# One block of ones for both buffers of k and v, value sums in three buffers in turn, and a new list of units, in an attention and bilinear kernel

## The chip, the cores and the metric

The kernel runs on one core of one Trainium2 chip. The metric is the device time of one execution in microseconds; a run gives one such time, and the profile is taken from one execution.

## The reference

```python
a    = exp(phi - max(phi, axis=2));  a = a / (sum(a, axis=2) + 1e-9)     # phi: 8 x 8 x 576 x 32
k_m  = einsum('bhsm,bhsd->bhmd', a, k);  v_m = einsum('bhsm,bhsd->bhmd', a, v)
attn = softmax(q @ k_m^T / sqrt(64))                                     # 576 x 32 for each batch and head
x    = (attn @ v_m).transpose(0, 2, 1, 3).reshape(4608, 512)
out  = ((x @ w_a) * (x @ w_b)) @ w_out                                   # 512 x 1536, 512 x 1536, 1536 x 512
```

There are 8 batches, 8 heads, 576 tokens, a head of 64, 32 memory slots; q, k and v are 8 x 8 x 576 x 64. Everything goes in and out as float32.

## The kernel before

The kernel keeps three weights in SBUF in half precision (`wa_sb`, `wb_sb`, `wo_sb`) and takes the eight batches one after the other, overlapped. Its work is cut into units, and a string `PLAN` lists all of them in one order. The kernel goes through that string, and each engine carries out its own instructions in the order in which the string brings them; nothing reorders them. So the list sets which instruction stands behind which on every engine and on POOL's DMA queue.

The tokens of the list are these (a leading digit is the batch).

- `w..`, `o`, `p`, `k`, `v`, `q` issue a load from POOL's queue: weights, `w_out`, phi, k, v, q.
- `exp` (ACT) is the exponential of phi. `kv` (`kv_sums`, PE, L323) multiplies it with k, v and a block of ones in one go of 72 matmuls on small tiles (192 columns: 64 of k, 64 of v, 64 equal sums), `km` (DVE) divides by the sums, `kvt` transposes (PE, DVE).
- `qt`/`qh` (DVE) transposes q, `sc`/`sh` (PE) gives scores, `e`/`eh` (ACT, L425) their exponentials `E`. Batches 0 to 3 are normalised with slots on partitions: `den` (PE L465, and the logarithm on ACT L466), `nr` (ACT L476, and the product `A`, L478, on DVE for batches 0 and 1 and on POOL for 2 and 3). Batches 4 to 7 transpose instead (`ed`, `sm`, `tn`, `ad`, DVE).
- `v{n}{a,b}` (`fold`, PE L516, small tiles) multiplies v_m with a third of `w_a` or `w_b`, and `x..` (`take_fold`, L548) copies the result to `vab`. So x itself is never built: an up product is `A` times `vab`.
- `a b.i.h` and `b b.i.h` (`up_half`) are the up products of row block i and half h of the tokens: two matmuls each (L727); `a` is copied by ACT (L731), `b` is multiplied with that copy by the DVE (L734) into `ht`.
- For batches 5 to 7 the first eight of twelve row blocks take both halves by seven products instead of eight: `P b.i.k` (`seven`, PE L750), k being the product's number. Products 1, 6, 7 and 4 are added up in one PSUM bank (y) in that order, 5 and 3 in a second (v), 2 alone in a third (x). ACT copies products 1, 5 and 6 out (`z`, L755), the DVE adds such a copy to products 3, 7 and 2 (`ah`, `bh`, `al`, L759) and multiplies product 4 (L777); `H` and `J` do the last multiplication on POOL or DVE (L781). These need sums of `vab` and of `A`: `S` (`v_sum`, L533) and `T` (`a_sum`, L541), with P or D at the end for POOL or DVE.
- The down products (`two_downs`, L654) do the same for two blocks of 128 tokens at a time: seven products of six matmuls of 256 columns; `d n` carries out the next n matmuls of them, 756 in all. They need sums of `ht`, `h` on POOL or `g` on DVE (`sum_tokens`, L638, 128x768), and of `wo_sb`, `T` on POOL or `V` on DVE without a leading batch (`sum_weights`, L621, 128x768). ACT copies (`u`, L661), the DVE adds and writes `o_sb` (L665), SP stores it.
- `O` and `M` write constants; `M` is the block of ones of the second buffer, by POOL (L792).

k and v of even batches lie in `kv_sbs[0]`, of odd ones in `kv_sbs[1]`, each of three planes: k, v, ones. The value sums have three tiles, one for each third of the weights' columns (`vsum0`, `vsum1`, `vsum2`); the transposed k_m and v_m of batch 0 and the reciprocals of batches 0 to 3 borrow two of these.

Of the kernel before, what the change touches and what calls it, by code (L numbers as in the profile page):

```python
# [8 lines left out]
F32 = mybir.dt.float32  # L9
F16 = mybir.dt.float16  # L10
# [3 lines left out]
P = 128  # L14
# [4 lines left out]
wb0:256 0qt0 wa0:256 0qt3 wb256:512 0qt1 wa256:512 p1 0exp0 0exp1 F1 0ks0 0kt0 0ks1 0vs1 0vt1 0vs0 0vt0 M k1 F1  # L19
0hv0a 0s0 v1 0qt2 O 0kt1 0e0 F1 0s1 0e1 0hx0a0 0hx0a1 F2 0den10 0den01 0den11 0den00 wa512:1024 0hv0b 0hx0b0 0hx0b1  # L20
0hv1b 0nr01 0nr10 0hx1b1 0nr11 0nr00 0hv1a 0hx1a0 q1.0 wb512:1024 0hx1a1 F4 a0.0.1 1exp1 a0.0.0 b0.0.0 0hx1b0 a0.1.1
b0.0.1 1exp0 a0.3.1 b0.1.1 a0.3.0 a0.2.0 b0.3.1 b0.2.0 a0.2.1 b0.2.1 1kv a0.1.0 1km1 wa1024:1536 1km0 b0.3.0 q1.1
1kvt 0v1a 0x1a0 0x1a1 1v0a 1v1a 1v0b 1x1a0 1x0a0 1x0b0 a0.5.1 1x1a1 1qh20 wb1024:1536 b0.1.0 o1 a0.6.0 1qh30 a0.4.0
1qh10 1qh00 o0 o3 1sh0 1eh00 0v1b 1v1b 1x0b1 1eh10 1x0a1 0x1b0 1den00 0x1b1 1x1b1 o4 1den10 o2 a0.6.1 b0.6.0 b0.6.1
b0.5.1 1nr10 1nr00 1x1b0 b0.4.0 a0.7.1 b0.7.1 a0.7.0 a0.5.0 b0.7.0 a1.5.0 b0.5.0 h0.3 b1.5.0 a1.3.0 1qh21 a0.4.1 o5
b1.3.0 1qh31 1qh01 a1.4.0 b0.4.1 a1.1.0 1qh11 a1.2.0 b1.4.0 a1.0.0 b1.1.0 1sh1 0v2a 1eh01 1eh11 0x2a1 b1.0.0 0x2a0
b1.2.0 1den01 a1.6.0 0v2b 0x2b0 0x2b1 b1.6.0 v2 a0.9.1 1v2b 1v2a 1x2b0 1x2b1 a0.11.1 1x2a1 1x2a0 b0.9.1 a0.10.1
a0.9.0 b0.11.1 b0.10.1 b0.9.0 V20 1den11 a1.10.0 b1.10.0 a0.11.0 b0.11.0 a0.8.0 a1.11.0 b0.8.0 b1.11.0 1nr11 d1
1nr01 a0.10.0 d1 V00 a1.8.0 b0.10.0 a1.7.0 d1 b1.8.0 p2 V21 a1.11.1 b1.7.0 b1.11.1 d1 a1.3.1 a1.0.1 a1.2.1 g0.0 d1
b1.3.1 a1.6.1 d1 b1.2.1 b1.0.1 V01 a0.8.1 V10 a1.4.1 a1.9.0 d1 k2 2exp0 2exp1 g0.1 d1 V11 b1.6.1 V31 a1.5.1 p3 g0.2  # L30
b0.8.1 q2 d1 b1.4.1 d3 a1.1.1 b1.9.0 d6 2kv 3exp0 k3 d2 2km0 d1 a1.9.1 2km1 v3 d3 b1.5.1 d1 3exp1 d1 a1.10.1 d2
a1.8.1 2kvt b1.1.1 d2 h1.0 a1.7.1 2qt1 d4 2qt0 2qt3 2v1b 2x1b1 2v0a 2x1b0 T30 2qt2 2x0a1 d12 2x0a0 d4 g2.0 g1.1 2sc
g1.2 2e0 b1.7.1 d1 2e1 g1.3 q3 d2 b1.8.1 d3 b1.10.1 d1 2den0 d1 g2.1 p5 2den1 d1 b1.9.1 d1 2nr0 d5 2v2b 3kv 2v1a
g2.3 2x2b1 3km0 2nr1 2x2b0 2x1a1 d7 3km1 d6 3qt2 2x1a0 2v0b 2v2a 2x0b1 3qt3 d3 3qt0 2x2a1 d3 a2.6.0 d1 b2.6.0 d1
3qt1 a2.4.0 2x2a0 b2.4.0 d1 h2.2 d1 a2.7.0 d2 a2.4.1 d1 2x0b0 b2.4.1 d4 a2.3.0 a2.1.1 3kvt 5exp1 v5 b2.7.0 p4 b2.3.0
a2.8.0 b2.1.1 k5 a2.1.0 d2 a2.2.0 d2 q4 d1 a2.5.0 h3.3 3sc 3e0 d2 b2.2.0 d1 3e1 d2 b2.8.0 5exp0 d1 b2.1.0 v4 d2
a2.10.0 d2 b2.10.0 a2.0.1 a2.11.0 b2.11.0 b2.5.0 3den0 a2.0.0 d1 b2.0.1 h3.0 d1 g3.1 a2.5.1 d1 a2.9.0 k4 b2.5.1 h3.2
b2.0.0 3nr0 a2.11.1 d1 a2.8.1 b2.9.0 d1 3den1 d2 a2.10.1 d2 b2.10.1 d1 3v0a 3nr1 3x0a1 5kv 3x0a0 3v0b 3x0b0 b2.8.1
a2.2.1 d1 q5 d1 4qt0 b2.11.1 4qt3 4exp1 d1 3x0b1 d3 b2.2.1 d1 a2.9.1 d1 4qt1 d2 4qt2 d1 a2.7.1 b2.9.1 g4.3 d1 a2.6.1
h4.0 a2.3.1 d1 g4.1 d1 a3.3.0 d1 h4.2 4exp0 k7 b2.7.1 a3.2.0 d2 b2.6.1 d5 b3.3.0 b3.2.0 d2 4kv p6 3v2a 4km0 d2 3x2a1  # L40
4km1 d11 3x2a0 b2.3.1 d2 4kvt d2 a3.0.0 a3.3.1 v6 5km0 q6 d2 a3.1.0 5km1 k6 h5.0 d5 b3.1.0 a3.1.1 4sc 4e0 b3.0.0 d1
5qt3 d2 b3.1.1 5qt0 d1 a3.0.1 4e1 d3 b3.3.1 d5 3v1b 3v1a 4ed 3v2b 3x1b1 d5 3x1a0 d2 3x1a1 4sm0 d1 5qt1 d2 h5.3 3x2b0
5kvt a3.8.0 4sm1 d1 3x1b0 h5.1 3x2b1 d4 5qt2 d3 a3.6.1 b3.0.1 a3.10.0 d3 a3.4.0 d1 p7 d1 6exp1 d1 b3.8.0 b3.4.0 d1
a3.5.0 b3.6.1 d1 b3.10.0 4tn1 a3.7.0 a3.9.0 h5.2 d1 5sc 4tn0 5e0 d1 b3.5.0 5e1 a3.5.1 a3.11.0 d1 b3.7.0 d3 6qt0 d4
4v0a 4x0a0 4v1b 4v0b 4x0b1 d2 4x1b1 d5 6qt2 d1 4ad d1 5ed d1 a3.4.1 5sm0 b3.5.1 d2 b3.9.0 d1 4x1b0 d3 4x0a1 b3.11.0
# [38 lines left out]
def kernel(  # L84
# [196 lines left out]
    def units(b):  # L281
# [269 lines left out]
        def one(f, *a):  # L551
            return lambda: f(*a)
# [289 lines left out]
```

## Time and profile before

| | |
|---|---|
| median of 3 runs | 234.72 us (234.55 to 235.18) |
| span of the profiled execution | 232.1 us |
| PE busy | 214.1 us, 92% of the span, 2906 matmuls |
| DVE busy | 195.7 us, 84% |
| ACT busy | 169.4 us, 73% |
| POOL busy | 138.2 us, 60% |
| read and written in HBM | 42.47 MB and 9.44 MB |

The profiled execution's own span is 232.1 us; the time of a run holds some 2.6 us more than the span. In the profile, PE is the matrix engine (PEld loads its weights), DVE the vector engine, ACT the scalar engine, POOL the GpSimd engine and SP the engine that issues the stores. A row of a timeline gives the start and the length in microseconds, the engine, the line of the kernel, the operation, output and input names and sizes, and in square brackets how long the engine had idled and what released it. Consecutive instructions of one kind are put together (x6); the start of the next row, not the sum of lengths, tells how far apart they are, for matmuls overlap. A row of the groups gives the number of instructions, their busy time, the mean of one in nanoseconds, and the idle time ahead of them.

### The profile page before, as it was taken

The numbers are of one execution on the slowest core, as the hardware profiler recorded it, in microseconds if no ns is written. First come the engines' busy times: TensorE is split into PE (matmuls) and PEld (weight loads), VectorE is DVE, ScalarE is ACT, GpSimd is POOL, SyncE is SP. The second block draws the span as 40 slices with busy tenths as digits, with TensorE's granted clock in tenths as the row PEclk, the third lists the DMA queues.
The fourth block names the chain that finished last, engine by engine and source line by source line (L and its number), as shares of the span: only waits on it lengthen the run. The fifth ranks groups of instructions, "written<-read, shape, count | busy, mean of one in ns | idle before, by whom it ended". The sixth has DMA issues, their size and how long they took to land.

```text
span 232.1 us, 7493 instructions
## 1 busy us (share of the span) xinstructions
PE 214.1 (92%) x2906; PEld 163.6 (70%) x2906; DVE 195.7 (84%) x517; ACT 169.4 (73%) x450; POOL 138.2 (60%) x139
## 2 busy tenths in 40 slices
PE   1189879999999998999999999999999999999993
PEld 0143537588778777777777787887778877888882
DVE  3543899999987667898988999999999999999942
ACT  2206679987899997589978996977897769785330
POOL 7927233812549597893374099499475991881151
PEclk9999999999999999999999999999999999999999
DMA  6999999999998999999840902121303303032164
GB/s 229 238 199 256 205 205 205 205 259 258 208 284 138 264 207 243 253 241 254 210 93 4 190 1 65 28 64 32 93 3 90 78 16 92 18 77 55 42 158 111
DMA packets 26259, 34.09 MB, mean 147 GB/s; under 512 B 2000, under 2 KB 20304, under 8 KB 26224
## 3 DMA queue, kind: packets, MB, share of 16 engines
q0 software_dynamic: 19760, 23.14, 53.5%
q1 hardware_dynamic: 5952, 9.70, 16.2%
q10 hardware_dynamic: 512, 0.79, 1.0%
q8 instruction: 22, 0.36, 0.6%
q14 instruction: 13, 0.11, 0.1%
HBM read 42.47 MB, written 9.44 MB: 224 GB/s over the span
## 4 chain that ended last, share of the span: by engine, by line
PE 71%; DMA 17%; POOL 6%; ACT 3%; issue 2%; DVE 1%; POOLq 0%
PE py L654 18%; PE pb L727 11%; PE pa L727 11%; PE pv L654 9%; DMA wb_sb<-in_moe_w_b_dram 6%; DMA kv_sb<-in_k_dram 6%; PE py L750 5%; PE px L654 4%; PE pva L516 4%; DMA kv_sb<-in_v_dram 4%; PE pv L750 3%; POOL h_sums L638 2%; PE pkv L323 2%; PE px L750 1%; ACT vab L548 1%
## 5 line engine op out<-in xcount | busy, mean ns | idle before, releaser
L734 DVE TENSOR_TENSOR ht<-a_sb,pb 128x288 f16<-128x288 f16 (+2 forms) x144 | 60.5, 445 | 9.6 <-PE pb L727 5.3
L727 PEld LDWEIGHTS <-vab 128*128 128x128 f16 x576 | 55.3, 98 | 14.9 <-issue 2.4
L731 ACT CAST a_sb<-pa 128x288 f16<-128x288 f32 (+2 forms) x144 | 55.1, 417 | 13.6 <-PE pa L727 8.9
L727 PE MATMUL pb<-A,vab 128*128 128x288 f16 (+2 forms) x288 | 54.9, 286 | 0.1
L727 PE MATMUL pa<-A,vab 128*128 128x288 f16 (+2 forms) x288 | 54.3, 286 | 0.5 <-DVE A L478 0.4
L548 ACT CAST vab<-pva 128x512 f16<-128x512 f32 x82 | 45.4, 611 | 6.9 <-PE pva L516 6.8
L654 PEld LDWEIGHTS <-h_sums 128*128 128x128 f16 x432 | 41.4, 98 | 9.9 <-issue 2.4
L638 POOL TENSOR_TENSOR h_sums<-ht 128x768 f16<-128x768 f16 x19 | 31.2, 1645 | 21.4 <-DVE ht L734 21.3
L654 PE MATMUL py<-w_sums,h_sums 128*128 128x256 f16 x216 | 38.1, 273 | 0.0
L654 PEld LDWEIGHTS <-ht 128*128 128x128 f16 x324 | 31.2, 98 | 7.5 <-issue 2.2
L654 PE MATMUL pv<-wo_sb,h_sums 128*128 128x256 f16 x216 | 36.4, 273 | 0.0
L638 POOL TENSOR_TENSOR h_sums<-ht,h_sums 128x768 f16<-128x768 f16 x10 | 16.4, 1640 | 11.6 <-DVE h_sums L638 11.5
L755 ACT COPY z<-py 128x288 f32<-128x288 f32 x48 | 19.2, 415 | 2.3 <-PE py L750 1.8
L781 POOL TENSOR_TENSOR ht<-ah,bh 128x288 f16<-128x288 f16 x19 | 13.7, 737 | 10.1 <-DVE ah L759 7.1
L654 PE MATMUL px<-wo_sb,ht 128*128 128x256 f16 x108 | 18.9, 273 | 0.0
L654 PE MATMUL py<-wo_sb,ht 128*128 128x256 f16 x108 | 18.8, 273 | 0.0
L654 PE MATMUL py<-w_sums,ht 128*128 128x256 f16 x108 | 18.4, 273 | 0.0
L661 ACT ACTIVATE u<-py 128x256 f32<-128x256 f32 x36 | 14.4, 399 | 4.0 <-PE py L654 3.9
L425 ACT ACTIVATE E<-pscore 128x288 f16<-128x288 f32 x28 | 9.8, 431 | 9.5 <-PE pscore L412 9.4
L291 ACT ACTIVATE exp_sb<-phi_sb 128x576 f16<-128x576 f32 x16 | 10.9, 692 | 5.2 <-DMA phi_sb<-in_phi_dram 5.2
L300 DVE STREAM_TRANSPOSE qT<-q_sb 128x288 f32<-128x288 f32 x28 | 12.2, 456 | 2.6 <-DMA q_sb<-in_q_dram 2.6
L750 PE MATMUL py<-asum,vab 128*128 128x288 f16 x48 | 13.5, 286 | 0.0
(106 smaller groups left out, 383.0 us busy)
## 6 DMA issues: line engine op xcount, KB each, us to landing
out_dram<-o_sb SPq DMA_DIRECT2D x68, 128.0 KB, 2.4
phi_sb<-in_phi_dram POOLq DMA_DIRECT2D x8, 576.0 KB, 10.3
kv_sb<-in_v_dram POOLq DMA_DIRECT2D x8, 576.0 KB, 11.2
kv_sb<-in_k_dram POOLq DMA_DIRECT2D x7, 576.0 KB, 13.5
q_sb<-in_q_dram POOLq DMA_DIRECT2D x6, 576.0 KB, 11.9
wo_sb<-in_moe_w_out_dram POOLq DMA_DIRECT2D x6, 256.0 KB, 14.0
wa_sb<-in_moe_w_a_dram POOLq DMA_DIRECT2D x2, 512.0 KB, 14.2
wb_sb<-in_moe_w_b_dram POOLq DMA_DIRECT2D x2, 512.0 KB, 16.6
```

The lines of the kernel that those rows point to most:

```text
L291: nc.scalar.activation(out=t["exp"][:, 2 * z:2 * z + 2, :, :], in_=phis[b][:, 2 * z:2 * z + 2, :].rearrange("p c (i m) -> p c i m", m=M), ...
L300: nc.vector.transpose(out=t["qT"][:, hp, :].bitcast(F32), in_=qs[b][:, hp, :].bitcast(F32))
L548: engine_copy(out=vabs[b][z][:, g, lo:hi], in_=pva[:, 0:hi - lo])
L638: engine.tensor_tensor(out=out, in0=in0, in1=in1, op=op)
L654: nc.tensor.matmul(po, lhs[:, i], rhs[:, i], start=first and i == 0, stop=i == KH - 1, skip_group_check=not first)
L661: nc.scalar.mul(out=x, in_=po, mul=scale)
L727: nc.tensor.matmul(ps, vabs[b][x][:, g, P * i:P * (i + 1)], attn[b][:, g, ts], start=(g == 0), stop=(g == 1))
L731: nc.scalar.copy(out=a_sbs[b, i, hf][:, :n], in_=ps)
L734: nc.vector.tensor_tensor(out=ht[:, i, t0:t0 + n], in0=a_sbs.pop((b, i, hf))[:, :n], in1=ps, op=ALU.mult)
L750: nc.tensor.matmul(x[bank][0], lhs, rhs, start=first, stop=True, skip_group_check=True)
L755: nc.scalar.copy(out=x[name], in_=po)
L781: engine.tensor_tensor(out=ht[:, i, t0 + HALF:t0 + S], in0=x["ah"], in1=x["bh"], op=ALU.mult)
```

## The change

There are three edits.

First, k and v of both buffers and one plane of ones lie in one tile of five planes, k0 v0 ones k1 v1. Each `kv` reads three neighbouring planes; in odd batches the ones come first, and `take_kv` picks the columns accordingly. The write of the second plane of ones (`M`) is gone.

Second, the value sums (and the two borrowers) take their tile from a pool of three buffers in turn.

Third, the list is new from end to end. The units are the same, but their order differs, and some sums change engine: `V20` and `V00` become `T20` and `T00` (POOL), the token sums on POOL go from 34 to 40, and of the 24 value sums POOL does 10 (12 before) and the DVE 14 (12). The helpers `part_sums`, `take_part` and `part_transpose` are added, and no token of the list calls them; `slot_sums`, which no token called, is removed.

```diff
 PLAN = """
-... 0vs1 0vt1 0vs0 0vt0 M k1 F1 0hv0a 0s0 v1 0qt2 O 0kt1 ...
+... 0vs1 0vt1 0vs0 0vt0 k1 F1 0hv0a 0s0 v1 0qt2 O 0kt1 ...
...
-... 1den11 a1.10.0 b1.10.0 a0.11.0 b0.11.0 a0.8.0 ... d1 V00 a1.8.0 b0.10.0
+... q2 a1.3.1 a1.4.1 T20 T00 2exp1 b1.0.1 b1.3.1 b1.4.1
...
-2den0 d1 g2.1 p5 2den1 d1 b1.9.1 d1 2nr0 d5 2v2b 3kv 2v1a g2.3 2x2b1 3km0 2nr1 2x2b0 ... 3qt0 2x2a1 d3 a2.6.0
-... 5exp1 v5 b2.7.0 p4 ... k5 a2.1.0 d2 a2.2.0 d2 q4 ... v4 d2 ... a2.9.0 k4 b2.5.1 h3.2
+2den0 2nr0 d8 2v2a 2x2a0 2v1a 2x1a1 3kv 3km0 2den1 2x1a0 2nr1 d3 k5 d2 3km1 2x2a1 d3 2v0b 2x0b1 2x0b0 2v2b
+d7 b1.10.1 d4 3qt3 d2 v5 k4 a2.0.1 3qt0 b2.0.1 ... 3v0b 3sc p4 3x0b1 3e1 v4 h3.0
...
+P6.6.3 H6.6 P6.6.2 d3 b6.8.0 d5 P6.5.5 P6.0.4 P6.5.1 P6.6.4 d3 7ad H6.0 a6.10.1 b6.11.0 h12.3 d2
+P6.5.6 P6.4.2 P6.4.6 d1 7T0P d2 P6.5.2 P6.5.7 a6.11.1 P6.5.3 d1 P6.4.5 H6.5 P6.4.7 b6.10.1
...
-b7.11.1 b7.9.1 d12 g15.2 g15.3 P7.2.3 b7.8.1 P7.3.3 d12 b7.10.1 d1 J7.3 H7.2 g16.0 d7 g16.1 g16.2 g16.3 g17.0 g17.1
-d2 h17.2 d20 h17.3 d66
+P7.3.3 b7.9.1 d14 b7.8.1 d5 H7.3 d9 b7.11.1 d11 H7.2 g16.0 g16.1 d12 g16.2 g16.3 d5 g17.3 d2 g17.0 d27 h17.1 d12 h17.2
+d24
 """
...
-    kv_sbs = [consts.tile([P, 3, NHP, NI * D], F16, name=f"kv_sb{t}") for t in range(2)]
-    kvs = [kv_sbs[b % 2] for b in range(B)]
+    kv_all = consts.tile([P, 5, NHP, NI * D], F16, name="kv_all")
+    kvs = [kv_all[:, 3 * (b % 2):3 * (b % 2) + 2] for b in range(B)]
+    trios = [kv_all[:, 2 * (b % 2):2 * (b % 2) + 3] for b in range(B)]
...
-    nc.vector.memset(kv_sbs[0][:, 2], 1.0 / CS)
+    nc.vector.memset(kv_all[:, 2], 1.0 / CS)
...
         def kv_sums():
...
-                            kvs[b][64 * r:64 * r + 64, 0:3 - given, hp, D * i:D * (i + 1)],
+                            trios[b][64 * r:64 * r + 64, :, hp, D * i:D * (i + 1)],
...
         def take_kv(gs=range(2)):
...
+            one, ks, vs = ((2, 0, 1), (0, 1, 2))[b % 2]
             for g in gs:
                 pkv, bank = t["pkv"][g]
-                nc.vector.reciprocal(out=t["rphi"][:, g:g + 1], in_=pkv[:, 2 * D:2 * D + 1])
-                km = pkv[:, 0:D].rearrange("p (d e) -> p e d", e=2).unsqueeze(2).to_broadcast([P, 2, 2, 32])
+                nc.vector.reciprocal(out=t["rphi"][:, g:g + 1], in_=pkv[:, one, 0:1])
+                km = pkv[:, ks].rearrange("p (d e) -> p e d", e=2).unsqueeze(2).to_broadcast([P, 2, 2, 32])
...
+    vpool = ctx.enter_context(tc.tile_pool(name="vpool", bufs=3))
...
-                both = spare.tile([P, 3, 512], F16, name="vsum1").rearrange("p z n -> p (z n)")
+                both = vpool.tile([P, 3, 512], F16, name="vsum").rearrange("p z n -> p (z n)")
...
-                vsums[b, n] = spare.tile([P, 3, 512], F16, name=f"vsum{n}")
+                vsums[b, n] = vpool.tile([P, 3, 512], F16, name="vsum")
...
-        elif x == "M":
-            nc.gpsimd.memset(kv_sbs[1][:, 2], 1.0 / CS)
```

More of the change, by code (lines that the diff above doesn't have):

```diff
@@ L24 @@
[L24 to L33, printed above, removed]
@@ new lines @@
+5x0a0 d1 a4.8.0 5T1P d4 5x1b0 d2 b4.8.0 d2 5S00D 5T3P g8.0 5S01D 5x1b1 a4.9.1 d5 5S11D a4.9.0 d3 P5.4.1 d1 b4.10.1
+b4.4.1 d2 7exp1 b4.9.1 P5.4.2 d3 7exp0 d1 5S21P d1 a4.0.0 b4.0.0 a4.6.0 b4.6.0 7qt3 5x0a1 h8.3 a4.8.1 d7 P5.5.1 b4.9.0
+a4.1.0 b4.1.0 P5.4.6 a4.10.0 5S10P d1 7qt2 a4.7.0 b4.7.0 P5.4.5 P5.4.7 a4.4.0 b4.4.0 6tn0 a4.1.1 d1 b4.1.1 d1 P5.4.4
+a4.2.0 g8.1 b4.2.0 d2 a4.6.1 P5.5.6 b4.10.0 a4.11.0 b4.11.0 P5.5.5 5S31P P5.4.3 a4.7.1 a4.5.0 b4.7.1 P5.5.7 h8.2
+a4.11.1 P5.5.2 P5.5.3 5v2b 5x2b0 5x2b1 5v2a 5S30D d3 P5.5.4 d1 5S20P d2 H5.5 5x2a1 5x2a0 d5 6sm1 b4.5.0 h9.0 d2 6tn1
@@ L306, in q_transpose_half @@
             nc.vector.transpose(out=t["qT"][:, hp, ts].bitcast(F32), in_=q_part(b, hf)[:, hp].bitcast(F32))
-        def slot_sums(z):
-            if z == 0:
-                t["es"] = kvs[b][:, 2, 0, 0:2 * NHP * M].bitcast(F32).rearrange("p (c m) -> p c m", m=M)
-            nc.vector.tensor_reduce(out=t["es"][:, 2 * z:2 * z + 2], in_=t["exp"][:, 2 * z:2 * z + 2].rearrange("p c i m -> p c m i"),
-                                    axis=mybir.AxisListType.X, op=ALU.add)
         def kv_sums():
-            given = "es" in t
-            n = (3 - given) * D
-            t["pkv"] = [banks.take([P, 2 * D + (1 if given else D)], F32, "pkv", hold=True) for _ in range(2)]
+            t["pkv"] = [banks.take([P, 3, D], F32, "pkv", hold=True) for _ in range(2)]
             for i in range(NI):
@@ L323, in kv_sums @@
                         nc.tensor.matmul(
-                            t["pkv"][g][0][32 * j:32 * j + 32, 0:n],
+                            t["pkv"][g][0][32 * j:32 * j + 32],
                             t["exp"][64 * r:64 * r + 64, hp, i, :],
-                            kvs[b][64 * r:64 * r + 64, 0:3 - given, hp, D * i:D * (i + 1)],
+                            trios[b][64 * r:64 * r + 64, :, hp, D * i:D * (i + 1)],
                             start=(i == 0),
@@ L330, in kv_sums @@
                         )
-            for g in range(2 * given):
-                for j in range(4):
-                    r, hp = head(g, j)
-                    nc.tensor.matmul(
-                        t["pkv"][g][0][32 * j:32 * j + 32, 2 * D:2 * D + 1],
-                        t["es"][64 * r:64 * r + 64, hp],
-                        one_cs[64 * r:64 * r + 64],
-                        start=True,
-                        stop=True,
-                        tile_position=(64 * r, 32 * j),
-                    )
         def take_kv(gs=range(2)):
@@ L352, in take_kv, with part_sums @@
                 half = slice(D * g, D * (g + 1))
                 for out, x in ((t["rep"][:, 0:2, half].rearrange("p e (z d) -> p e z d", z=2), km),
-                               (t["rep"][:, 2, half], pkv[:, D:2 * D])):
+                               (t["rep"][:, 2, half], pkv[:, vs])):
                     nc.vector.tensor_scalar(out=out, in0=x, scalar1=t["rphi"][:, g:g + 1], scalar2=None, op0=ALU.mult)
                 banks.free(bank)
+        def part_sums(x):
+            planes = ((slice(0, 3, 2), slice(1, 2)), (slice(0, 2), slice(2, 3)))[b % 2][x]
+            t["part", x] = [banks.take([P, 2 - x, D], F32, "pkv", hold=True) for _ in range(2)]
+            for i in range(NI):
+                for g in range(2):
+                    for j in range(4):
+                        r, hp = head(g, j)
+                        nc.tensor.matmul(
+                            t["part", x][g][0][32 * j:32 * j + 32],
+                            t["exp"][64 * r:64 * r + 64, hp, i, :],
+                            trios[b][64 * r:64 * r + 64, planes, hp, D * i:D * (i + 1)],
+                            start=(i == 0),
+                            stop=(i == NI - 1),
+                            tile_position=(64 * r, 32 * j),
+                        )
@@ new lines, in take_part @@
+        def take_part(x, g):
+            if "rep" not in t:
+                t["rep"] = spare.tile([P, 3, P], F16, name="rep")
+                t["rphi"] = small.tile([P, 2], F32, name="rphi")
+            pkv, bank = t["part", x][g]
+            half = slice(D * g, D * (g + 1))
+            if x == 0:
+                one, ks = ((1, 0), (0, 1))[b % 2]
+                nc.vector.reciprocal(out=t["rphi"][:, g:g + 1], in_=pkv[:, one, 0:1])
+                km = pkv[:, ks].rearrange("p (d e) -> p e d", e=2).unsqueeze(2).to_broadcast([P, 2, 2, 32])
+                out = t["rep"][:, 0:2, half].rearrange("p e (z d) -> p e z d", z=2)
+            else:
+                km, out = pkv[:, 0], t["rep"][:, 2, half]
+            nc.vector.tensor_scalar(out=out, in0=km, scalar1=t["rphi"][:, g:g + 1], scalar2=None, op0=ALU.mult)
+            banks.free(bank)
@@ L358, in kv_transpose, with part_transpose @@
+        def part_transpose(x):
+            if "kvT" not in t:
+                t["kvT"] = mid.tile([P, 3, P], F16, name="kvT")
+            xs = (slice(0, 2), slice(2, 3))[x]
+            pT = banks.tile([P, 2 - x, P], F16, name="pT")
+            for y in range(2 - x):
+                nc.tensor.transpose(out=pT[:, y, :], in_=t["rep"][:, 2 * x + y], identity=ident)
+            nc.vector.tensor_copy(out=t["kvT"][:, xs], in_=pT)
         def kv_transpose():
@@ L370, in sums @@
                 t["rphi"] = small.tile([P, 2], F32, name="rphi")
-                t["kvT"] = spare.tile([P, 3, 512], F16, name="vsum0").rearrange("p z n -> p (z n)")[:, :6 * P].rearrange("p (x n) -> p x n", n=P)
+                t["kvT"] = vpool.tile([P, 3, 512], F16, name="vsum").rearrange("p z n -> p (z n)")[:, :6 * P].rearrange("p (x n) -> p x n", n=P)
             part = (slice(0, 3, 2), slice(1, 2))[x]
@@ L555, in units @@
             u[f"exp{z}"] = one(exp_phi, z)
-            u[f"ps{z}"] = one(slot_sums, z)
+            u[f"{'kv'[z]}p"] = one(part_sums, z)
+            u[f"{'kv'[z]}x"] = one(part_transpose, z)
+            for g in range(2):
+                u[f"{'kv'[z]}g{g}"] = one(take_part, z, g)
             u[f"ks{z}"] = one(sums, z, 0)
```

102 lines of the change are left out of this document (52 added, 50 removed).

## The prediction

> **What bounds the kernel now.** I read the page first: the busy line and the slices.
>
> ```profile
> span 232.1 us, 7493 instructions
> PE 214.1 (92%) x2906; PEld 163.6 (70%) x2906; DVE 195.7 (84%) x517; ACT 169.4 (73%) x450; POOL 138.2 (60%) x139
> PE   1189879999999998999999999999999999999993
> ```
>
> TensorE is the bound, but not evenly: only the first six slices and the last are loose. The windows cut the span there (columns: stretch, its length, busy us and count of PE, PEld, DVE, ACT, POOL, the granted clock, DMA share, GB/s).
>
> ```profile
> 0.00:35.00 35.00, 21.61 (x442) 11.07 (x442) 20.53 (x57) 14.90 (x38) 20.00 (x31) 1.00 1.16 222
> 35.00:228.20 193.20, 192.52 (x2466) 152.52 (x2464) 174.78 (x461) 154.54 (x413) 118.17 (x108) 1.00 0.64 134
> 120.00:215.00 95.00, 95.00 (x1044) 76.54 (x1043) 92.27 (x244) 77.13 (x210) 60.68 (x57) 1.00 0.26 58
> ```
>
> From 35 to 228.2 us PE misses 0.68 of 193.20 us, and in the 95 us that hold the seven-product units it misses nothing, at clock 1.00. The number of matmuls is the same in both kernels, so there is a floor close below, and almost all that can happen is a new wait. The PE timeline names the four waits left from 29 us on.
>
> ```profile
> 29.52 0.42 PE L363 MATMUL pT<-ident,rep 128*128 128x128 f16 x3 [0.74 <-DVE rep L355]
> 33.15 0.36 PE L442 MATMUL pscore<-qT,kvT 32*32 32x160 f16 x32 [0.55 <-DVE qT L306]
> 33.71 0.41 PE L516 MATMUL pva<-wb_sb,vsum 64*32 64x512 f16 x8 [0.19 <-DMA wb_sb<-in_moe_w_b_dram]
> 92.30 0.61 PE L323 MATMUL pkv<-kv_sb,exp_sb 64*32 64x192 f16 x40 [0.59 <-DMA kv_sb<-in_k_dram]
> ```
>
> The profiled execution spans 232.1 us; the median of the runs is 234.72 us, 2.6 us more, lying around the span. I take these 2.6 us as unchanged, and what follows the last matmul too: both lists end in downs alone. So the sum is made as a difference, onto 234.72.
>
> **The layout and the memset.** GpSimd's write of the ones goes (POOL timeline):
>
> ```profile
> 9.22 2.06 POOL L792 MEMSET kv_sb<- 128x2304 f16 x1
> 11.18 0.77 POOL L155 DMA_DIRECT2D kv_sb<-in_k_dram  x1
> 16.88 0.31 POOL L260 TENSOR_SCALAR_AFFINE_SELECT ones<-ones 128x128 f16<-128x128 f16 x1 [4.19 <-DVE ones L259]
> ```
>
> It frees 2.06 us on POOL at 9.22, and the next two issues can go earlier. But POOL then idles 4.19 us for the DVE anyway, so everything issued behind 16.88 stays where it is, and the transfers ahead of it already fill 0 to 35 us at 222 GB/s. The weights whose wait ends at 33.71 are issued behind it. I book nothing; what the start could give at most is a rival below. The odd batches' other order of pkv's columns and the pool of three for the value sums change no instruction's size: nothing.
>
> **The loads.** The stall at 92.30 comes from POOL's order (POOL timeline, then the piece of the chain of waits):
>
> ```profile
> 76.27 1.65 POOL L638 TENSOR_TENSOR h_sums<-ht 128x768 f16<-128x768 f16 x1
> 77.85 0.77 POOL L155 DMA_DIRECT2D kv_sb<-in_k_dram  x1
> 77.85 14.31 DMA kv_sb<-in_k_dram
> ```
>
> k4 is issued at 77.85, behind a chain of GpSimd sums, and lands at 92.16. In the new list k4 stands right behind v5, ahead of the first up product of batch 2, 11 us of PE work earlier than before, and ahead of p4, v4 and q5; 4kv keeps its place on PE within 0.1 us. Even if POOL issues it only 4 us earlier it lands at 88. The 0.59 us go. v4 now goes after p4; by the same queue it lands some 4 us later than k4, still ahead. What is late next is the A of batch 2:
>
> ```profile
> 64.56 0.41 PE L465 MATMUL pD<-E,ones 128*128 128x288 f16 x2
> 64.53 1.32 ACT L466 ACTIVATE asum<-pD 128x288 f32<-128x288 f32 x4
> 67.00 0.74 ACT L476 ACTIVATE vsum<-asum 128x576 f16<-128x576 f32 x1
> 66.77 2.52 POOL L478 TENSOR_TENSOR A<-E,vsum 128x576 f16<-128x576 f16 x2 [5.40 <-ACT vsum L476]
> ```
>
> From the denominators at 64.56 to the second A at 69.29 are 4.73 us; PE had 5.35 us of other work in between (the sum of its start-to-start steps from 2den1 to a2.6.0). The new list has 3.40 us from 2den1 to a2.0.1. With nothing queued between, the same chain is 1.29 (64.56 to 65.85, the logarithms) + 0.74 + 1.26 (half of 2.52) + some 0.2 of handing over = 3.5. So 0.1 us is short, and 1.33 if the queues are as before. I take 0.1, as 2nr0 now stands ahead of 2den1 and the first A is out of the way.
>
> **The order of the seven products.** Products 6, 3 and 7 are added onto products 1, 5 and 6 in the same PSUM bank, so each must wait until ACT has copied the earlier one out (z); product 4 waits in the same way until the DVE has read product 7 (bh). In the trace (PE, then ACT and DVE, the chain's steps, the group of copies):
>
> ```profile
> 208.71 0.29 PE L750 MATMUL py<-asum,vab 128*128 128x288 f16 x1
> 208.96 0.29 PE L750 MATMUL py<-asum,vsum 128*128 128x288 f16 x1
> 209.08 0.29 PE L750 MATMUL pv<-asum,vsum 128*128 128x288 f16 x1
> 209.28 0.40 ACT L755 COPY z<-py 128x288 f32<-128x288 f32 x1 [0.30 <-PE py L750]
> 209.58 0.41 ACT L755 COPY z<-pv 128x288 f32<-128x288 f32 x1
> 209.24 0.45 DVE L759 TENSOR_TENSOR bh<-py,z 128x288 f16<-128x288 f32 x1
> 213.13 0.49 PE pa L727 x4
> 214.11 0.66 PE pv L654 x6
> L755 ACT COPY z<-py 128x288 f32<-128x288 f32 x48 | 19.2, 415 | 2.3 <-PE py L750 1.8
> ```
>
> From the matmul's start to the copy's end is 209.68 − 208.96 = 0.72 with a free ACT, and 209.99 − 209.08 = 0.91 right behind another copy. Over all 72 copies (48 in the row above, 24 from pv) it is 0.72 to 1.41, median 0.78. PE meanwhile streams 0.1225 us (0.49/4) for a matmul of 288 columns and 0.11 (0.66/6) for one of 256. Adding these steps between the partners gives how much cover each has. In the old list the shortest covers are 1.16 (1 to 6), 1.17 (6 to 7) and 1.20 us (5 to 3): the copy is always in. In the new one 12 of the 72 are under 1.0 and 24 under 1.2, the shortest 0.82. For P6.5.6 to P6.5.7 the list runs "P6.5.6 P6.4.2 P6.4.6 d1 7T0P d2 P6.5.2 P6.5.7": four of .1225 and three of .11, 0.82. With 0.05 for the handing over, a copy at the median needs 0.83 and just fits; one behind another copy waits 0.14. Setting each of the 72 covers against the 72 delays measured, the expected wait is 0.64 us in all (0.07 for the old list). It is 0 if ACT is free at every tight place, and 3.2 us if each needed 1.1. I take 0.64, since ACT is busy 77.13 of 95 us there and seldom free. From product 7 at 208.71 to the end of bh at 209.69 are 0.98 us; two of the 24 pairs 7 to 4 now have 0.89 and 0.97 (the shortest before 1.25): 0.15.
>
> **The sums that change engine.** Net, six sums of tokens and two of weights go from DVE to GpSimd, two sums of values the other way.
>
> ```profile
> L638 POOL TENSOR_TENSOR h_sums<-ht 128x768 f16<-128x768 f16 x19 | 31.2, 1645 | 21.4 <-DVE ht L734 21.3
> L638 DVE TENSOR_TENSOR h_sums<-ht 128x768 f16<-128x768 f16 x17 | 9.2, 549 | 0.1
> L533 POOL TENSOR_TENSOR vsum<-vsum,vab 128x512 f16<-128x512 f16 x3 | 3.5, 1152 | 0.1
> L533 DVE TENSOR_TENSOR vsum<-vsum,vab 128x512 f16<-128x512 f16 x3 | 1.2, 416 | 0.0
> ```
>
> DVE loses 8 × 0.549 − 2 × 0.416 = 3.6 us of 195.7; POOL gains 8 × 1.645 − 2 × 1.152 − 2.06 = 8.8 us on 138.2. POOL has the room, DVE was never what PE waited for behind 35 us, and most sums are read many units later: 0. The end is the exception. Behind its last up product (b7.11.1) the new list has 93 steps of downs, the old one 96 behind b7.10.1. In them come six sums on DVE (g16.0 to g17.0) and then h17.1 and h17.2 in a row on POOL, where the old list makes g17.1 on the DVE and has only h17.2 on POOL before these are needed. Counted from b7.11.1: 0.9 us to ht (about the 0.98 of bh above), one output sum of 0.4, six sums of 0.5 gives 4.3, two of 1.645 gives 7.6; PE needs h17.2 after 69 steps, 0.25 + 69 × 0.11 = 7.8. So it fits by 0.2; a DVE that comes half a microsecond late costs 0.3. I take +0.1, between 0 and 0.6.
>
> The new list also has one more change between small and full tiles on PE (25 groups for 24). Going in costs 83.94 − 83.73 = 0.21 us where a 256-column step takes 0.11, and coming out about as much: +0.2, between 0 and 0.4.
>
> ```profile
> 83.73 0.27 PE L654 MATMUL px<-wo_sb,ht 128*128 128x256 f16 x1
> 83.94 0.41 PE L516 MATMUL pva<-wa_sb,kvT 64*32 64x512 f16 x8
> ```
>
> Sum: −0.59 (k4) + 0.10 (A) + 0.64 + 0.15 (products) + 0.10 (end) + 0.20 (tiles) = +0.60, so 234.72 + 0.60 = 235.3 us.
>
> **The rivals.**
>
> Slower, copies that queue. If the closer pairs meet on ACT, each late copy pushes the next product, its copy, and the next again; the delay's median goes from 0.78 towards 1.1 and the waits to 3.2 us: 235.3 − 0.64 + 1.6 to 3.2, about 236.3 to 237.9. It decides from a median of about 0.95. For it: ACT's 81% there and the 9 of 72 copies that took over 0.95 already. Against: the old list's PE lost nothing in those 95 us.
>
> Slower, DVE held by GpSimd. Eight more GpSimd pieces of 1.645 us that read the same SBUF as DVE's sums. If each held the DVE once for half its length it would cost 8 × 0.82 = 6.6 us, against 3.6 taken off DVE and 95.00 − 92.27 = 2.7 free there: 0.3 us over, and with two of them in a bad place 2 × 0.82 more: 235.6 to 237.2. It decides once more than 6.3 us are held. Against: the 0.1 us idle ahead of the DVE's 17 sums shows no such hold, with 34 sums on GpSimd.
> The Trainium skill, page "SBUF — State Buffer", section "SBUF: two separate sides", states this as an exclusive lock: a DVE operation with two SBUF inputs and a GpSimd operation that reads SBUF exclude each other for the whole instruction. By that rule the eight moves would be worth less than their 3.6 us; the trace neither shows a held DVE nor rules one out.
>
> Faster, the start fills. The waits at 29.52, 33.15 and 33.71 are 1.48 us. If the new order puts other ready work there, half of it goes, and with free copies the result is 234.72 − 0.59 − 0.74 + 0.2 = 233.6; if all is covered but the start stays, 234.3, or 234.1 with nothing for the tiles. Against it: the first units run in nearly the same order in both lists, and the third wait ends with a transfer.
>
> No effect as said: with k0 v0 ones k1 v1 in one tile a load of k1 could wait for the matmuls that read the ones or the other half. Each wait would then be a load late by up to a unit, 2 us or more, 237. Against: accesses are tracked by region, and k1, v1 share none with k0, v0.
>
> **How the numbers follow.** About 0.3% (0.7 us) is what a measurement of this kernel can tell from no change: 234.02 and 235.42 are the limits. Forecast, with new waits of 0.2 to 1.5 us beside the tiles: 234.5 to 235.8, chance 0.46 (0.26 same, 0.20 slower). All covered, 234.1 to 234.3: 0.12 (0.10 same, 0.02 faster). The start fills, 233.4 to 234.1: 0.16 (0.14 faster, 0.02 same). Copies that queue: 0.17 slower. DVE held: 0.07 slower. False waits: 0.02 slower. That makes 0.16 faster, 0.38 same, 0.46 slower. The range runs from 233.7 (about half of the filled start) to 236.9 (most of the queueing copies and of the held DVE).
>
> **What would show it.** Right: no wait before the kv products of batch 4; PE's timeline from 130 us on with small gaps put to z (ACT) ahead of products 7 and 3 of batches 5 to 7, 0.2 to 1.2 us in all; DVE 192 and POOL 147 us busy; the three waits of the start nearly unchanged. Wrong: PE without a gap in that stretch (then ACT was free at each tight pair), gaps above 2 us, an idle DVE ahead of its sums, or a start that is shorter or longer by over 0.4 us.

## The result and the profile after

The changed kernel takes 244.18 us (242.82 to 245.38) where the one before, run beside it, takes 234.63 us: a ratio of 1.0414, 95% interval 1.0359 to 1.047. It is 9.5 us slower; the forecast was 235.3 us and the range ended at 236.9. The profiled execution took 242.82 us, its span is 240.9 us, 8.8 more than before. The page of the changed kernel, the three lines shown of before:

```profile
span 240.9 us, 7497 instructions
PE 216.4 (90%) x2906; PEld 163.1 (68%) x2906; DVE 203.6 (85%) x511; ACT 170.5 (71%) x450; POOL 149.7 (62%) x144
PE   1288889987999999999799999999996999999993
```

The slices of PE have new dents in the middle. DVE has six instructions fewer and is busy 7.9 us longer, where the sum had it 3.6 us shorter: that is the line that does not fit. The windows of the changed kernel (columns as before):

```profile
0.00:35.00 35.00, 21.79 (x444) 11.05 (x445) 20.59 (x57) 15.06 (x39) 18.04 (x30) 1.00 1.16 222
35.00:70.00 35.00, 32.61 (x501) 23.97 (x501) 32.73 (x80) 28.55 (x80) 20.86 (x19) 1.00 1.20 228
70.00:100.00 30.00, 30.00 (x472) 23.47 (x470) 23.00 (x66) 25.54 (x68) 18.44 (x18) 1.00 1.10 227
100.00:130.00 30.00, 28.06 (x403) 21.82 (x408) 27.33 (x62) 24.05 (x62) 18.79 (x16) 1.00 0.84 168
130.00:160.00 30.00, 29.40 (x312) 23.15 (x313) 28.49 (x70) 25.31 (x68) 23.80 (x20) 1.00 0.16 36
160.00:190.00 30.00, 27.86 (x369) 21.44 (x367) 29.12 (x72) 22.08 (x59) 22.26 (x19) 1.00 0.24 55
190.00:230.00 40.00, 40.00 (x375) 32.68 (x373) 39.15 (x103) 28.33 (x77) 23.02 (x23) 1.00 0.27 63
```

PE loses 2.39, 1.94, 0.60 and 2.14 us in four windows and nothing in the two others behind 35 us, at clock 1.00. The start is as before (21.79 us busy for 21.61), the end too: the last matmul starts at 236.44 instead of 227.84, 8.60 us later, and the span ends 8.8 later. These four losses make 7.07 us; as recorded matmuls overlap, a wait costs a little more than the idle time shown, and the shortest ones show only as longer busy time (PE is busy 2.3 us more for the same 2906 matmuls). The waits view of the changed kernel (who waited for whom, total, times, longest; four lines of it) names the DVE, and two rows of PE's timeline show where:

```profile
PE pb L755 <- DVE ht L762: 3.7, 2, 1.9
PE py L778 <- DVE bh L787: 1.6, 1, 1.6
PE px L778 <- DVE ht L762: 0.6, 1, 0.6
PE pv L682 <- ACT u L689: 0.4, 1, 0.4
55.22 0.43 PE L755 MATMUL pb<-A,vab 128*128 128x320 f16 x2 [1.81 <-DVE ht L762]
185.06 0.28 PE L778 MATMUL py<-asum,vab 128*128 128x288 f16 x1 [1.62 <-DVE bh L787]
```

What made the DVE late stands ahead of the instruction named. Here are DVE's and POOL's timelines at the last large wait (PE's at 185.06), then around the first (PE's at 55.22):

```profile
180.75 0.68 DVE L666 TENSOR_TENSOR h_sums<-ht 128x768 f16<-128x768 f16 x1
181.35 1.64 DVE L527 TENSOR_TENSOR E<-E,sum 128x512 f16<-128x512 f16 x1
182.91 1.73 DVE L809 TENSOR_TENSOR ht<-ah,bh 128x288 f16<-128x288 f16 x1
184.56 0.45 DVE L787 TENSOR_TENSOR bh<-py,z 128x288 f16<-128x288 f32 x1
181.09 1.35 POOL L558 TENSOR_TENSOR vsum<-vab,vsum 128x512 f16<-128x512 f16 x1
182.40 2.08 POOL L666 TENSOR_TENSOR h_sums<-h_sums,ht 128x768 f16<-128x768 f16 x1
51.81 2.44 DVE L649 TENSOR_TENSOR w_sums<-wo_sb 128x768 f16<-128x768 f16 x1
52.17 1.65 POOL L666 TENSOR_TENSOR h_sums<-h_sums,ht 128x768 f16<-128x768 f16 x1
```

A last multiplication of 288 columns (at 182.91) takes 1.73 us and ends 0.17 us after GpSimd's sum of tokens does (184.64 and 184.47); a sum of weights (at 51.81) takes 2.44 us and ends 0.43 after GpSimd's sum of tokens. The GpSimd piece is stretched too when the DVE came first (2.08 for 1.645 us). So it looks as if one of the two waits for the other; I call such an instruction held. The waiting is inside the recorded length of an instruction, so the page counts it as busy and no idle time appears. Two of the groups that carry it, of the changed kernel, and the same two of the one before:

```profile
L527 DVE TENSOR_TENSOR E<-E,sum 128x512 f16<-128x512 f16 x4 | 6.5, 1623 | 0.0
L809 DVE TENSOR_TENSOR ht<-ah,bh 128x288 f16<-128x288 f16 x5 | 4.4, 875 | 0.0
L502 DVE TENSOR_TENSOR E<-E,sum 128x512 f16<-128x512 f16 x4 | 2.7, 682 | 0.0
L781 DVE TENSOR_TENSOR ht<-ah,bh 128x288 f16<-128x288 f16 x5 | 1.5, 298 | 0.0
```

As held time I take each instruction's length above the shortest of its kind in any run, if over 0.12 us and after the first 20 us. The kernel before has none; the changed one has nine on DVE, 11.3 us in all, 2.6 us the longest, and nine on POOL, 2.6 us. All nine on DVE have both inputs in SBUF and lie across a GpSimd addition or product. The old kernel has 79 such DVE instructions, and not one overlaps a GpSimd addition or product; the new one has 73, and 20 overlap. Such an overlap is called a meeting from here on. The DVE instructions with an input in PSUM overlap about as often in both, 194 and 189 of 294, and keep their usual length (the products into `ht` take 444 ns, 445 before).

### The profile page after: what moved, and what is told of

It is laid out like the page before. It is cut to its first block, busy times and chain, and to the rows that moved or that the text cites. A ratio compares the mean times of both kernels' runs of the same rounds, so it can differ in the third digit from the quotient of the medians.

```text
span 240.9 us, 7497 instructions
## 1 busy us (share of the span) xinstructions
PE 216.4 (90%) x2906; PEld 163.1 (68%) x2906; DVE 203.6 (85%) x511; ACT 170.5 (71%) x450; POOL 149.7 (62%) x144
## 4 chain that ended last, share of the span: by engine, by line
PE 78%; DVE 11%; DMA 4%; ACT 2%; issue 2%; POOL 1%; DVEq 0%; POOLq 0%
PE py L682 18%; PE pb L755 14%; PE pa L755 13%; PE pv L682 8%; PE py L778 5%; PE pva L541 5%; PE px L682 5%; DMA kv_all<-in_v_dram 4%; PE pv L778 3%; DVE ht L762 2%; PE pkv L314 2%; PE pscore L437 1%; DVE E L527 1%; PE px L778 1%; DVE w_sums L649 1%
## 5 line engine op out<-in xcount | busy, mean ns | idle before, releaser
L759 ACT CAST a_sb<-pa 128x288 f16<-128x288 f32 (+2 forms) x144 | 55.8, 414 | 20.4 <-PE pa L755 10.8
L755 PE MATMUL pb<-A,vab 128*128 128x288 f16 (+2 forms) x288 | 55.8, 286 | 3.9 <-DVE ht L762 3.7
L755 PE MATMUL pa<-A,vab 128*128 128x288 f16 (+2 forms) x288 | 55.7, 286 | 0.5 <-DVE A L503 0.4
L666 POOL TENSOR_TENSOR h_sums<-ht 128x768 f16<-128x768 f16 x19 | 32.0, 1685 | 9.3 <-DVE ht L762 9.2
L682 PE MATMUL pv<-wo_sb,h_sums 128*128 128x256 f16 x216 | 34.8, 273 | 0.4 <-ACT u L689 0.4
L682 PE MATMUL py<-w_sums,h_sums 128*128 128x256 f16 x216 | 34.7, 273 | 0.0
L666 POOL TENSOR_TENSOR h_sums<-h_sums,ht 128x768 f16<-128x768 f16 x11 | 19.1, 1740 | 8.0 <-DVE h_sums L666 7.7
L682 PE MATMUL px<-wo_sb,ht 128*128 128x256 f16 x108 | 18.3, 273 | 0.0
```

The lines of the kernel that those rows point to most:

```text
L666: engine.tensor_tensor(out=out, in0=in0, in1=in1, op=op)
L682: nc.tensor.matmul(po, lhs[:, i], rhs[:, i], start=first and i == 0, stop=i == KH - 1, skip_group_check=not first)
L755: nc.tensor.matmul(ps, vabs[b][x][:, g, P * i:P * (i + 1)], attn[b][:, g, ts], start=(g == 0), stop=(g == 1))
L759: nc.scalar.copy(out=a_sbs[b, i, hf][:, :n], in_=ps)
```

## Experiments

The theory is that the 9.5 us come from such meetings. The rivals: the new layout and buffers make something wait; the new order itself makes PE wait. A third rival, that sums moved to GpSimd come too late for those who read them, finds nothing in the changed kernel's trace: no wait of PE and no idle time of a DVE group there ends with POOL. The table gives the time and its ratio to the kernel before, run beside it, and the held DVE instructions of the profiled execution.

| run | us | ratio (95%) | held on DVE: count, us |
|---|---|---|---|
| changed kernel | 244.18 | 1.041 (1.036 to 1.047) | 9, 11.3 |
| new code, old list | 234.16 | 1.000 (0.996 to 1.004) | 0 |
| new list, seven sums on the other engine | 240.42 | 1.027 (1.018 to 1.036) | 6, 6.1 |
| new list, twelve on the other engine | 237.94 | 1.013 (1.009 to 1.018) | 3, 1.2 |
| new list, GpSimd sums read nothing | 234.01 | 0.998 (0.995 to 1.000) | 2, 0.6 |
| old order, new list's engines | 244.10 | 1.042 (1.035 to 1.049) | 14, 11.5 |
| new order, old list's engines | 251.38 | 1.072 (1.063 to 1.080) | 14, 13.7 |
| old list, eight GpSimd additions added | 247.38 | 1.056 (1.049 to 1.063) | 9, 10.2 |
| old list, eight GpSimd memsets added | 240.61 | 1.027 (1.022 to 1.033) | 1, 1.0 |

**The code without the list.** The edit to the changed kernel:

```diff
 PLAN = """
-(the new list)
+(the old list without M)
```

> The code of the changed kernel (five planes, value sums in three buffers in turn) with the old list, M dropped. Theory: the 9.5 us come from the new list, in which two-input DVE instructions meet GpSimd instructions and are held (11.4 us of lengthened DVE instructions in the changed kernel's trace, none in the old one). Then this kernel is at 234.6 us, within 0.7, with no lengthened DVE instruction. Rival (layout): loads or sums wait on the shared tile or on the buffers in turn; then most of the 9.5 us appear here, 240 us or more.

It measured 234.16 us, ratio 1.000 with an interval of 0.4% to either side, and DVE's sums are at their old length:

```profile
span 231.6 us, 7492 instructions
L668 DVE TENSOR_TENSOR h_sums<-ht,h_sums 128x768 f16<-128x768 f16 x8 | 4.4, 553 | 0.1
```

Within that interval the tile of five planes, the value sums in turn and the memset dropped cost nothing and bring nothing. The layout rival falls, and with it the false waits of the prediction. All 9.5 us are the list's.

**Meetings taken away by moving sums.** The edit:

```diff
-h0.1 ... T30 ... h5.2 ... h9.0 ... 6S01P ... 6S31P ... h12.1
+g0.1 ... V30 ... g5.2 ... g9.0 ... 6S01D ... 6S31D ... g12.1
```

> The new list with seven sums on the other engine, so that the DVE instructions that were held most no longer meet a GpSimd one: h0.1, h5.2, h9.0, h12.1 as g, T30 as V30, 6S01P and 6S31P as D. DVE gets 3.6 us more work by the rows. Theory (holding): most of the PE waits of 1.97, 0.60, 2.10, 0.77, 0.41 and 1.79 us go; 236 to 239 us, some new meeting included as everything behind moves. Rival (order): the waits come from the order of the units; with more work on DVE it is as slow or slower, 243 to 246.

240.42 us, 1.4 us above the expected range: better than the changed kernel by 3.8 us with, by the rows, 3.6 us more work given to DVE, so the order rival's 243 or more is out, but six meetings are left, some of them new (a product `A` of 0.29 us now takes 1.66, across T20). Everything behind a removed wait moves, and other pairs meet. Five more moves, taken from that trace:

```diff
-T20 T00 ... h6.1 ... J5.4 ... h11.3
+V20 V00 ... g6.1 ... H5.4 ... g11.3
```

> The new list with the seven sums moved as before and five more, taken from the meetings left in that run's trace: T20 and T00 as V20 and V00, h6.1 and h11.3 as g, J5.4 as H5.4. Theory (holding): DVE lengthening falls from 5.8 us to under 3, and the time from 240.4 to 235.5 to 238. Rival (order): 240 to 243, with the added DVE work of 1.9 us.

237.94 us: inside the expected range, with 1.2 us held. The 3.3 us that remain above the old kernel are not all held time; PE's waits there are small ones, at most 0.35 us of idle time each, all but one for a DVE that now does 11 sums more and one multiplication less than in the changed kernel. That rest I did not follow further.

**Meetings taken away without moving anything.** All GpSimd sums and last multiplications keep their place in the list and their output, but read nothing:

```diff
+    def combine(engine, out, in0, in1, op):
+        if engine is nc.gpsimd:
+            for _ in range(2):
+                nc.gpsimd.memset(out, 0.5)
+        else:
+            engine.tensor_tensor(out=out, in0=in0, in1=in1, op=op)
...
-            engine.tensor_tensor(out=out, in0=in0, in1=in1, op=op)
+            combine(engine, out, in0, in1, op)
```

> The new list as it is; every GpSimd sum (of tokens, of values, of A, of weights) and every GpSimd last multiplication is replaced by two memsets of its output, about 1.4 us for the sum of tokens instead of 1.645, which read nothing and wait for no input: the values computed are left out. The GpSimd additions of batch 4 to 7's normalising and of A stay. Theory (holding): the lengthened DVE instructions of the changed kernel go but for those that meet the ones that stay (0.3 to 0.8 us), and with them PE's waits: 233.8 to 235.5 us. Rival (order): waits of 1.5 us and more stay and the time is 241 or more.

234.01 us, ratio 0.998 (0.995 to 1.000). The windows of that run:

```profile
35.00:70.00 35.00, 34.98 (x534) 26.06 (x534) 31.55 (x87) 31.41 (x86) 20.57 (x28) 1.00 1.20 239
70.00:130.00 60.00, 60.00 (x918) 46.78 (x916) 50.08 (x131) 51.09 (x134) 41.10 (x60) 1.00 0.95 196
130.00:190.00 60.00, 60.00 (x670) 48.06 (x668) 57.43 (x153) 49.46 (x134) 40.58 (x78) 1.00 0.21 49
```

PE misses 0.02 of 155 us, and DVE takes 139.06 us there where the old kernel's three windows give 141.15. In this run the new order of matmuls, copies and loads makes PE wait for nothing: the order rival falls. As the memsets are shorter than the sums and wait for no input, this bounds what the new list could reach and is no version of the kernel.

**Meetings added to the old list.** To the first of these runs (new code, old list), eight times, next to a sum of tokens on DVE:

```diff
+        elif x == "Z":
+            nc.vector.memset(sx[:, 0:1], 1.0)
+        elif x == "X":
+            sy = sx[:, 680:1360]
+            nc.gpsimd.tensor_tensor(out=sy, in0=sx[:, 0:680], in1=sy, op=ALU.add)
+        elif x == "Y":
+            nc.gpsimd.memset(sx, 1.0)
```

`sx` is a buffer of its own, filled once near the start. Z releases X, or Y in the second kernel; its place in the list is just ahead of the DVE's sum, or one or two DVE instructions earlier.

> The old list on the new code with eight GpSimd additions added (128x680, both inputs in SBUF, result unused), each released just ahead of, or one or two instructions ahead of, a DVE sum of tokens, where POOL was idle. Theory (holding): each such DVE sum of 0.55 us takes 1.0 to 2.0 us; 6 to 10 us more DVE time, of which PE feels 2 to 7: 237 to 242 us. Rival (no holding, only POOL's own queue): DVE durations stay 0.55; 234.5 to 235.5.

> As the run before, with a GpSimd memset of 128x1360 (about 1.2 us, reads nothing) in place of each addition. If only a GpSimd instruction that reads SBUF excludes the DVE's two-input one, DVE durations stay 0.55 and the time 234.5 to 235.5; if any GpSimd compute instruction does, it is 236 to 241 with the sums at 1.0 to 1.7 us.

247.38 and 240.61 us, both above what was expected. The DVE's sums of tokens, first with additions, then with memsets:

```profile
L668 DVE TENSOR_TENSOR h_sums<-ht 128x768 f16<-128x768 f16 x17 | 14.1, 839 | 0.1
L668 DVE TENSOR_TENSOR h_sums<-ht 128x768 f16<-128x768 f16 x17 | 9.2, 552 | 0.1
```

With additions six sums of tokens are held and take 1.70 to 1.84 us; the three others held there are a sum of weights, one of values and a product `E`. With memsets the sums of tokens keep their 0.55. So a GpSimd addition that reads SBUF holds them, and a memset, which only writes, does not. The memset run is nevertheless 6.4 us slower than its base, and more than half of that has nothing to do with holding: POOL waits for the marker (Z) with the issue of batch 2's k behind it, at 52.93 where the base issues it at 42.53, and batch 4's k comes late as well (0.9 us). Both runs lose some 3 us at the first (PE timeline, additions, then memsets):

```profile
59.33 0.94 PE L316 MATMUL pkv<-kv_all,exp_sb 64*32 64x192 f16 x72 [3.45 <-issue]
58.77 1.64 PE L316 MATMUL pkv<-kv_all,exp_sb 64*32 64x192 f16 x72 [2.99 <-issue]
```

The difference between the two is 6.8 us, with 9.2 us more held on DVE; not all of it need be the hold, as an addition also keeps POOL longer than a memset (1.2 us).

**The two halves of the list.** Of the sums and last multiplications 40 change engine (the expectation counted 38). The first run has the old order with the new engines, the second the new order with the old ones. The first's edit against the old list (the second's is the reverse, on the new list):

```diff
-V20 ... V00 ... g0.1 ... g2.1 ... h3.2 ... h4.0 ... 5S00P ... J5.5
+T20 ... T00 ... h0.1 ... h2.1 ... g3.2 ... g4.0 ... 5S00D ... H5.5
```

> The old order on the new code, each sum and last multiplication on the engine that the new list gives it (38 of them differ; net six sums of tokens and two of weights more on GpSimd, two of values less). Prediction's premise: moving eight net sums to GpSimd costs nothing, 234.5 to 235.5. Holding by place: what counts is who meets whom; the old order was free of meetings only with its own engines, so some 3 to 8 meetings of 0.5 to 1.5 us, 236 to 241.

> The new order on the new code, each sum and last multiplication on the engine that the old list gives it. Prediction's premise (the engines matter little): about as the changed kernel without holds, 234 to 235. Holding by number of GpSimd pieces: fewer meetings in proportion, 242. Holding by place: again 3 to 10 meetings, 236 to 244; that this and the run before both are well above the old kernel would say that neither half is the cause by itself, but the fit of the two.

244.10 and 251.38 us, both above what was expected: each half alone is as bad as both, or worse. In the first the sums of this form, eight in either kernel, take 1008 ns instead of 553; in the second a PE wait of 1.42 us ends with a sum of tokens:

```profile
L668 DVE TENSOR_TENSOR h_sums<-ht,h_sums 128x768 f16<-128x768 f16 x8 | 8.1, 1008 | 1.6 <-POOL h_sums L668 1.5
59.26 0.28 PE L682 MATMUL py<-w_sums,h_sums 128*128 128x256 f16 x1 [1.42 <-DVE h_sums L666]
```

The second has the old number of sums of tokens on GpSimd, 34, and is the slowest of all: the number doesn't decide, the fit of order and engines does. The old list is free of meetings only as a whole. In these two runs not all of the time is holding: DVE also waits for sums and products of GpSimd, 2.0 us in the first and 2.5 in the second, and of the second's 16.8 us above the old kernel only 13.7 are held. That rest was not followed.

**The meeting by itself.** Nothing of the reference is computed; idle engines, one stretch after the other:

```diff
+    def g():
+        nc.vector.tensor_tensor(out=od, in0=x, in1=y, op=ALU.add)
+    def T(second=False):
+        nc.gpsimd.tensor_tensor(out=(og, os)[second], in0=x, in1=z[:, 0:N], op=ALU.add)
+    def D():
+        nc.gpsimd.dma_start(out=w[:, 0:1536], in_=wa[:, 0, :])
+    def M():
+        nc.gpsimd.memset(z, 1.0)
```

> The cost by itself: nothing of the reference is computed. Thirteen short stretches on idle engines, each released by ACT: DVE additions of 128x768 with both inputs in SBUF, or DVE products of 128x288 with one input in PSUM, beside a GpSimd addition of 128x768, two of them, one behind a DMA issue, a DMA issue alone, or a memset. Theory: the two-input addition (0.55 us) that starts inside a GpSimd addition ends 0.5 us after that one's end; with the DVE first the GpSimd addition is longer instead; with PSUM input, a memset or a DMA issue alone nothing is longer. From two rows of the changed kernel (the DVE from 51.81 and from 110.44): with a GpSimd addition ready behind a DMA issue, a DVE addition that starts during the issue ends only after that second addition.

In turn: GpSimd first; the DVE first; a DMA issue running; an issue with a GpSimd addition ready behind it; a memset (DVE's and POOL's timelines, each POOL row behind its DVE row):

```profile
8.94 1.67 DVE L70 TENSOR_TENSOR od<-x,y 128x768 f16<-128x768 f16 x1
8.56 1.63 POOL L76 TENSOR_TENSOR og<-x,z 128x768 f16<-128x768 f16 x1 [0.47 <-ACT w L85]
13.40 0.56 DVE L70 TENSOR_TENSOR od<-x,y 128x768 f16<-128x768 f16 x1 [0.32 <-ACT x L87]
13.60 1.84 POOL L76 TENSOR_TENSOR og<-x,z 128x768 f16<-128x768 f16 x1 [0.93 <-ACT w L85]
49.47 0.56 DVE L70 TENSOR_TENSOR od<-x,y 128x768 f16<-128x768 f16 x1
49.06 0.57 POOL L79 DMA_DIRECT2D w<-in_moe_w_a_dram  x1 [3.33 <-ACT x L91]
43.90 2.24 DVE L70 TENSOR_TENSOR od<-x,y 128x768 f16<-128x768 f16 x1
43.49 0.57 POOL L79 DMA_DIRECT2D w<-in_moe_w_a_dram  x1 [2.97 <-ACT x L91]
44.08 1.64 POOL L76 TENSOR_TENSOR og<-x,z 128x768 f16<-128x768 f16 x1
54.88 0.56 DVE L70 TENSOR_TENSOR od<-x,y 128x768 f16<-128x768 f16 x1
54.39 2.01 POOL L82 MEMSET z<- 128x2304 f16 x1 [4.77 <-ACT x L91]
```

With GpSimd first the DVE's addition ends at 10.61, 0.42 after GpSimd's (10.19). With the DVE first it keeps its 0.56 us and GpSimd's is 0.21 longer. An issue or a memset alone holds nothing. DVE's products with one input in PSUM, in the other stretches, take 0.45 us beside a GpSimd addition and without one. The stretch from 43.90 is told of at the end.

## Why the prediction was wrong

The step that failed is the term "The sums that change engine ... 0", together with the price and the chance of the rival "DVE held by GpSimd" (0.07, at most 237.2 us). That rival's mechanism is the one that decided. The run with the old order and the new engines measures the term by itself: 9.5 us where it had 0. Three things in its working were wrong.

- It priced the eight pieces moved, net, each with half its length. But 40 pieces changed engine and the order was new too, so each of the 73 two-input DVE instructions could meet any GpSimd sum: 20 did, nine were held by more than 0.12 us, by 1.25 us on average and by up to 2.6 us where two GpSimd pieces followed each other.
- It set the held time against DVE's free time as a whole (6.3 us). A wait of PE depends on the one place: the 2.44 us sum at 51.81 made a PE wait of 1.81 us at 55.22, though DVE idles 2.3 us in the window from 35 to 70.
- It took the 0.1 us idle ahead of the DVE's 17 sums as evidence against holding. A hold is inside the recorded length, so idle time could not have shown it. The lengths were short too (549 ns), but none of 79 such instructions met a GpSimd one, while 194 of 294 with an input in PSUM did. That was in the old trace, and says that meetings were absent, not that they are free.

The Trainium skill, page "SBUF — State Buffer", section "SBUF: two separate sides", has the rule: whoever of the two starts first keeps the shared port for its whole instruction, and only a GpSimd operation that reads SBUF counts against a two-input DVE one. The changed kernel's rows agree (1.73 us for 0.30), as do the memset run (552 ns) and the stretches from 8.56 and 13.40. The stretch from 43.90 does not: there the DVE started first, by the record, and was held, and the measurement decides.

Of the other terms:

- k4: right. The kv of batch 4 at 89.20 has no wait in the changed kernel (0.59 us before).
- The A of batch 2 (0.1): no wait.
- The seven products (0.64 and 0.15): nothing by themselves. No PE wait names `z`; the wait at 185.06 is one of a product 4 for `bh`, but behind a held multiplication. With only 0.6 us held (the memsets in place of GpSimd's sums) PE misses 0.02 of 155 us. Copies took 0.72 to 1.30 us, median 0.78, much as before; at the tightest place 0.05 us was left (cover 0.83, delay 0.78). The delays were set against the covers as if independent, and they were not: at the five tightest places the copies took 0.72 to 0.78. These 0.79 us were not there.
- The end (0.1): no wait; the 93 steps of downs behind the last up product run through.
- The tiles (0.2): not measured by themselves, so that term stays open.
- The start: its three waits are 0.74, 0.29 and 0.35 us where they were 0.74, 0.55 and 0.19, so neither filled nor lengthened.

Without the holding the run nearest to the new list gave 234.01 us, about the "all covered, 234.1 to 234.3" that had 0.12. So it is luck that the forecast had the right sign: the terms that made its sum positive were not there, and what made the kernel slower stood in it with 0.

## What to carry to other kernels

Where the DVE and GpSimd share sums over SBUF, count in the trace how many two-input DVE instructions overlap a GpSimd one: none of many is a sign that the order keeps them apart, and any new order or swap of engines must then be priced by its meetings: here 20 overlaps held nine instructions, by 0.2 to 2.6 us each and 1.25 on average. Look for them as instructions longer than the shortest of their kind, since the wait is recorded as busy time. To move pieces away from single meetings helps slowly (244.2, 240.4, 237.9 us), as it makes new ones; order and engines have to be chosen together, with the meetings counted.

## What the runs showed of the hardware

Holding seems to depend on what is ready behind a DMA issue on POOL. In the stretch by itself the DVE's addition started at 43.90, 0.18 us ahead of GpSimd's at 44.08, and still waited for it: 2.24 us, to 46.14, 0.42 after GpSimd's end. With the plain order (13.40 and 13.60) the DVE kept its length, and with an issue alone (49.06) too. The changed kernel has two rows like it: the sum at 51.81 (its GpSimd addition, ready behind an issue, is recorded from 52.17), and a normalising product at 110.44, which took 3.31 us. That one starts inside a GpSimd product, outlasts the issue behind it and ends only after the next GpSimd addition (DVE, then POOL):

```profile
110.44 3.31 DVE L527 TENSOR_TENSOR E<-E,sum 128x512 f16<-128x512 f16 x1
109.53 1.27 POOL L527 TENSOR_TENSOR E<-E,sum 128x640 f16<-128x640 f16 x1
110.74 0.79 POOL L157 DMA_DIRECT2D kv_all<-in_v_dram  x1
111.55 1.65 POOL L666 TENSOR_TENSOR h_sums<-ht,h_sums 128x768 f16<-128x768 f16 x1
```

So a GpSimd addition seems to have the port from before its recorded start when it stands ready behind an issue; one stretch and two rows show it, and why was not tried further.
